# A planned attention and feed-forward kernel: transfers become work of two servers, three pairs' sums go by way of rows in memory, and the ranks are new

## The chip, the core and the metric

The kernel runs on one core of a Trainium2 chip. The metric is the device time of one execution in microseconds; lower is better. A core has five engines that each run their own list of instructions in order: PE (matrix products), DVE (vector), ACT (activation functions), POOL (a slower vector engine that here issues the weights' transfers) and SP (it computes nothing here and issues the other transfers). 16 DMA engines carry the data of all queues.

## The reference, cut to what matters

```python
# q, k, v: (8, 8, 576, 64) float32; moe_w_in: (512, 2048), moe_w_out: (2048, 512), float64
scores = (q @ k.T) / 8
thresh = scores.max(-1) - tau
scores = where(scores >= thresh, scores, -1e9)
attn   = exp(scores - scores.max(-1)); attn /= attn.sum(-1) + 1e-9
x      = (attn @ v)                    # put together to (4608, 512)
h      = x @ w_in
out    = (h * sigmoid(1.702 * h)) @ w_out
```

## The kernel before

**Pairs and blocks.** The 64 heads are 32 pairs, numbered 0 to 31; four pairs make the 512 columns of one batch's x. The feed-forward part takes blocks of 256 tokens. The first two blocks use plain products (`mm1_0`, L754, and `mm2`, L735); blocks from 2 on use products of a fast matrix scheme (`mm1` and `product`); the last four have a scheme of their own.

**What happens to a pair n.**
1. SP loads q and k (`load_qk`, L359) and v (`load_v`, L372). DVE transposes q and k (`prep`, L474).
2. PE makes nine score tiles (`scores`, L489), ACT copies each out of PSUM (`keep`, L506), two to a stored tile, so that a pair has four full tiles and a half one.
3. DVE takes maxima (`in_groups`, L512, once for each tile; `over_tiles`, L522; `over_halves`, L532). For all pairs but pair 2 the row of thresholds is then turned (`turn_rows`, L551), written to device memory by SP (`row_out`, L563) and read back spread over the partitions (`row_in`, L571). Pair 2 is spread by DVE (`spread_max`). Below, "the row's trip" is the way from `row_out` to the landing of `row_in`.
4. DVE subtracts the row from each tile (`sub`, L578); ACT masks it (`mask`, L584) and takes exponentials (`exps`, L588).
5. PE multiplies by v (`values`, L607). The sums of the exponentials of pairs 0 to 4 come from PE (`sums_by_pe`, L615, and `one_row`, L628); from pair 5 on DVE adds them (`in_groups` again, then `over_tiles`). For pairs 5 to 7 DVE then brings them into place and spreads them (`one_group`, L639, and `spread_sums`, L681); from pair 8 on they take a trip through memory like the maxima (`turn_sums`, L653, `sums_out`, L665, `sums_in`, L672).
6. DVE multiplies and puts the result into x (`place_x`, L691).

**Weights.** They come as float64 and are turned into float32 on the chip, in 32 pieces, 16 of `moe_w_in` and then 16 of `moe_w_out`. POOL issues two copies of each piece (L428, the words, and L429, the same bytes shifted by three), DVE cuts out the exponent (`cv_ex`, L437) and the fraction (`cv_frac`, L449, two instructions), ACT makes the power of two (`cv_power`, L444), DVE multiplies both (`cv_end`, L462). A piece needs a staging place, and the place comes free with the `cv_end` of an earlier piece: among the pieces of `moe_w_out` there are one place that pieces 16, 19, 22 and 25 use in turn, and two that the others alternate between. The first six loads wait for `hold` of pair 2 or 3, which follows that pair's `prep`.

**What orders the work.** Nothing is ordered by a scheduler on the chip. A planner in Python (`run_in_order`, L243) plays the program through: a list of tasks, each with an engine, a cost, a rank, the tasks that it comes after, the buffers that it takes and gives back, and a lag (the time after its end at which other engines see it). An idle engine takes the ready task of the lowest rank. A task's rank is its pair's number plus a bias from a table by the function's name (`EARLY` for pairs 0 to 3, `SECOND` for 4 to 7, `LATER`, and `CV` for the weights). The order that comes out is the order of issue, so a wait at the head of an engine's list holds all that is behind it. Before, a transfer is a task of the engine that issues it, with a long lag for the flight: 9.0 for a weight piece, 3.3 and 5.2 for the two halves of a row's trip, 3.0 to 10.0 for q and k.

**First feed-forward product.** `mm1_0` of hidden block 0 can start when `place_x` of pairs 0 to 3 is done and weight pieces 0 to 3 are converted. From there PE has feed-forward work to fill the time between attention work. The planner holds feed-forward products at the lowest priority and gates the scores of pair n by them.

Of the kernel before, what the change touches and what calls it, by code (L numbers as in the profile page):

```python
# [10 lines left out]
FP32 = mybir.dt.float32  # L11
# [3 lines left out]
AF = mybir.ActivationFunctionType  # L15
ALU = mybir.AluOpType
# [3 lines left out]
P = 128  # L20
# [10 lines left out]
def kernel(  # L31
# [84 lines left out]
    stop = const.tile([P, 1], FP32, name="stop")  # L116
    shift = const.tile([P, 1], FP32, name="shift")
# [9 lines left out]
    for x in ("raw0", "raw1", "qkT0", "qkT1", "mb"):  # L127
# [6 lines left out]
        "exps": -11.47,  # L134
        "in_groups": 5.75,
        "keep": 10.66,
        "load_qk": -0.27,
        "load_v": 4.86,
        "mask": -2.66,
        "one_group": -15.86,  # L140
        "one_row": 12.67,
        "over_halves": -7.01,
        "over_tiles": -4.01,
        "place_x": -17.11,
        "prep": -11.73,
        "row_in": 20.49,
        "row_out": 4.47,
        "scores_run": 12.45,
        "spread_max": -1.73,
        "spread_sums": 7.14,  # L150
        "sub": 9.27,
        "sums_by_pe": 0.27,
        "sums_in": -9.39,
        "sums_out": 2.13,
        "turn_rows": -12.55,
        "turn_sums": -0.41,
        "values": 14.64,
        "w_sum": 4.11,
        "x_sum": -14.1,
    }  # L160
    SECOND = {
        "exps": -7.29,
        "in_groups": 20.95,
        "keep": 16.67,
        "load_qk": -8.88,
        "load_v": 5.53,
        "mask": 2.36,
        "one_group": 2.55,
        "one_row": -2.71,
        "over_halves": -12.07,  # L170
        "over_tiles": 2.86,
        "place_x": -20.26,
        "prep": 3.49,
        "row_in": -19.42,
        "row_out": -24.08,
        "scores_run": -7.99,
        "spread_max": -3.11,
        "spread_sums": -2.29,
        "sub": 14.98,
        "sums_by_pe": 35.93,  # L180
        "sums_in": 7.43,
        "sums_out": 4.05,
        "turn_rows": -3.84,
        "turn_sums": 4.03,
        "values": 11.79,
        "w_sum": -10.45,
        "x_sum": -10.98,
    }
    LATER = {
        "exps": 2.01,  # L190
        "in_groups": 10.37,
        "keep": -0.02,
        "load_qk": -6.6,
        "load_v": 3.77,
        "mask": 14.79,
        "one_group": 4.78,
        "one_row": -14.98,
        "over_halves": 1.09,
        "over_tiles": -6.27,
        "place_x": -0.34,  # L200
        "prep": 2.34,
        "row_in": 4.02,
        "row_out": 2.64,
        "scores_run": -11.25,
        "spread_max": -9.44,
        "spread_sums": -6.73,
        "sub": 2.14,
        "sums_by_pe": 1.46,
        "sums_in": 3.78,
        "sums_out": 2.16,  # L210
        "turn_rows": 12.26,
        "turn_sums": 0.29,
        "values": -10.38,
        "w_sum": 6.61,
        "x_sum": 6.02,
    }
    CV = {
        "cv_end": -8.05,
        "cv_ex": 2.22,
        "cv_frac": -11.72,  # L220
        "cv_power": -4.72,
        "load_w": -7.79,
    }

    LAG = {"PE": 0.26, "DVE": 0.18, "ACT": 0.22, "POOL": 0.18}

    QUARTERS = ("scores", "scores_run", "values", "sums_by_pe")
# [12 lines left out]
    FIRST, LAST = -9.0, 1000.0  # L240
    need, follows = {}, {}

    def run_in_order():  # L243
# [12 lines left out]
        while events:  # L256
# [18 lines left out]
            for engine, queue in ready.items():  # L275
                if engine in busy:
                    continue
                for rank, i in sorted(queue):
# [25 lines left out]
    JOINT = 7  # L304

# [183 lines left out]
    def scores(n, j):  # L489
# [8 lines left out]
        if j == NK - 1:  # L498
            del mats[n, 0], mats[n, 1]
# [32 lines left out]
    def over_halves(n):  # L532
        r = stats[n, ALU.max]
        o = work.tile([P, QB], FP32, name="fold", tag="fold", bufs=1)
        for x in (1, 3) if n in BY_DMA else range(4):
            nc.vector.tensor_scalar(
                out=o[ts(x ^ 1, 32)], in0=r[ts(x, 32)], scalar1=gap[ts(x, 32)], scalar2=None,
                op0=ALU.subtract,
            )
        if n in BY_DMA:  # L540
# [10 lines left out]
    def turn_rows(n):  # L551

        nc.vector.transpose(out=flat[1], in_=flat[0])

# [23 lines left out]
    def sub(n, t):  # L578
        s = sT[n, t].rearrange("p u h s -> p u (h s)")
        nc.vector.tensor_tensor(  # L580
# [26 lines left out]
    def values(n, tiles):  # L607
# [4 lines left out]
        if n < NPAIR:  # L612
            free_scores(n, tiles)
# [333 lines left out]
    nc.gpsimd.memset(ones, 1.0)  # L947
    nc.gpsimd.dma_start(
# [26 lines left out]
    BY_PE = 5  # L975
    BY_DMA = (0, 1, *range(3, NP))
    SUMS_BY_DMA = range(8, NP)
    LEAD = 6
    WHOLE = 6

    FFU = 1.727
    T_RANK = FIRST

    W_RANK = (0, 12.87, 12.51, 22.24, 0, 4.97)
    ready_w, w_loads, w64 = [], [], 0
    for i in range(len(pieces)):
# [10 lines left out]
        a = task("POOL", 1.1, rank, load_w, i, after=w_loads[-1:], take=place, lag=9.0)  # L997
        w_loads.append(a)
        e = task("DVE", 0.345, rank, cv_ex, i, after=[a])
        m = task("ACT", 0.67, rank, cv_power, i, after=[e])  # L1000
        a = task("DVE", 1.1, rank, cv_frac, i, after=[e])

        over = [ready_w[y] for y in range(i) if i >= n_in and stage(y) == (i - n_in) // PER_STAGE]
        ready_w.append(task("DVE", 0.61, rank, cv_end, i, after=[a, m] + over, give=place))
# [191 lines left out]
    for n in range(NP):  # L1196
# [5 lines left out]
        slow = 1.1 if n < NPAIR else 1.0  # L1202
# [3 lines left out]
        cost = 3.5 if NPAIR <= n < 2 * NPAIR else 2.0  # L1206
        lag = (4.6, 3.0)[n] if n < 2 else 10.0 if n < 2 * NPAIR else 3.0
        lq = task("SP", cost, r - 2.0, load_qk, n, 0, q0, after=behind, take=own(n, "raw0"), lag=lag)
        lk = task(
            "SP", cost if n else 0.1, r - 2.0, load_qk, n, 1, q1, after=behind,  # L1210
            take=own(n, "raw1"), lag=lag,
        )
        v_m = f"v_m{n % 2}"
        lv = task("SP", 2.4, r + (1.85 if n < 2 else -1.2), load_v, n, after=lvs[-1:], take=(v_m,), lag=3.0)
# [161 lines left out]
```

## Time and profile before

| What | us |
|---|---|
| median of 3 runs (lowest to highest) | 1318.74 (1318.22 to 1318.92) |
| profiled execution, its own time | 1317.94 |
| its span, first to last instruction | 1316.2 |
| PE busy in the span | 1260.9 |
| DVE busy | 1006.1 |
| ACT busy | 646.6 |
| POOL busy | 249.0 |

The profiled execution lies 0.80 us under the median, and 1.74 us of it are outside the span. The page splits the span into 40 slices of 32.9 us and gives each engine's busy share of a slice in tenths. The view by windows gives the same in microseconds for stretches that one names. The timeline gives instructions in order of time, with the idle time in front of them and what ended it in brackets. An engine name with a q (SPq, POOLq) is the engine's sequencer, which issues transfers.

### The profile page before, as it was taken

What the parts mean: (1) busy time and instruction counts of PE and PEld (TensorE: products, weight loads), DVE (VectorE), ACT (ScalarE), POOL (GpSimd) and SP (SyncE); (2) the same over time, 40 slices, a digit from 0 to 9 for tenths busy, and PEclk for the clock granted to TensorE, in tenths of its full rate; (3) what the DMA queues carried; (4) which work ended last, traced back from release to release, by engine and by line L of the source; (5) the groups of instructions that cost most, each with busy time, mean ns of one, the idle gap of its engine ahead of it and who ended that gap; (6) DMA issues with size and microseconds to landing.
All of it is one profiled execution on the core that took longest, in us unless ns stands there. A gap on an engine that the chain in (4) does not pass through costs nothing. (4 is left out here: it accounts for less than half of the span.)

```text
span 1316.2 us, 22807 instructions
## 1 busy us (share of the span) xinstructions
PE 1260.9 (96%) x9128; PEld 975.6 (74%) x9128; DVE 1006.1 (76%) x1610; ACT 646.6 (49%) x830; POOL 249.0 (19%) x291
## 2 busy tenths in 40 slices
PE   5669999999999999999999999999999999999998
PEld 2346864457887777777778888777777778888887
DVE  7989999898888887788777877777888863652642
ACT  4876666576554555555554555454556540210210
POOL 1201211012031211213021303030212117120120
PEclk8879999999999999999999999999999999999999
DMA  8976766545323223212213222323122110000000
GB/s 152 293 189 207 230 207 149 112 77 100 85 55 71 55 55 71 51 50 54 58 42 72 55 71 55 71 55 71 36 55 54 36 46 8 9 1 25 8 0 32
DMA packets 258819, 102.88 MB, mean 78 GB/s; under 512 B 233754, under 2 KB 243994, under 8 KB 258714
## 3 DMA queue, kind: packets, MB, share of 16 engines
q1 hardware_dynamic: 244986, 63.40, 22.4%
q0 software_dynamic: 11360, 37.74, 9.3%
q8 instruction: 71, 1.16, 0.4%
q10 hardware_dynamic: 2368, 0.30, 0.2%
q14 instruction: 34, 0.28, 0.1%
HBM read 87.51 MB, written 9.69 MB: 74 GB/s over the span
## 5 line engine op out<-in xcount | busy, mean ns | idle before, releaser
L516 DVE TRANSPOSE_TENSOR_REDUCE part<-arena 128x36 f32<-128x1152 f32 (+1 forms) x295 | 357.5, 1235 | 41.9 <-ACT arena L510 32.4
L718 PE MATMUL hps<-xT,w_in 128*128 128x256 f32 x1536 | 337.2, 380 | 0.5 <-DVE arena L730 0.4
L718 PEld LDWEIGHTS hps<-xT,w_in 128*128 128x128 f32 x1536 | 290.7, 190 | 45.9 <-issue 5.7
L586 ACT ACTIVATE arena<-arena 128x1152 f32<-128x1152 f32 (+1 forms) x160 | 169.4, 1059 | 144.0 <-DVE arena L580 143.8
L510 ACT COPY arena<-ps 128x576 f32<-128x576 f32 x288 | 170.7, 647 | 115.3 <-PE ps L493 111.9
L580 DVE TENSOR_TENSOR arena<-arena 128x1152 f32<-128x1152 f32 (+1 forms) x158 | 201.1, 1313 | 20.5 <-DMA arena<-row 20.5
L909 PE MATMUL ops<-w_out,arena 128*128 128x256 f32 x896 | 202.4, 380 | 1.8 <-DVE arena L730 1.8
L590 ACT ACTIVATE arena<-arena,shift,scl 128x1152 f32<-128x1152 f32 (+1 forms) x160 | 200.3, 1252 | 4.1
L493 PE MATMUL ps<-arena 64*64 64x288 f32 x2304 | 174.7, 420 | 22.9 <-DVE arena L477 15.3
L909 PEld LDWEIGHTS ops<-w_out,arena 128*128 128x128 f32 x896 | 169.3, 190 | 28.7 <-DVE arena L730 3.1
L875 POOL TENSOR_TENSOR arena<-arena 128x256 f32<-128x256 f32 x56 | 49.7, 888 | 647.1 <-DVE arena L730 543.9
L601 PE MATMUL pv<-arena 64*64 64x288 f32 x2176 | 159.7, 408 | 0.0
L727 ACT ACTIVATE th<-hps 128x512 f32<-128x512 f32 x112 | 66.0, 589 | 186.0 <-PE hps L718 171.8
L909 PE MATMUL ops<-arena 128*128 128x256 f32 x672 | 150.7, 380 | 0.7 <-DVE osb L931 0.7
L493 PEld LDWEIGHTS ps<-arena 64*64 64x64 f32 x2304 | 84.0, 137 | 90.8 <-ACT arena L510 30.4
L909 PEld LDWEIGHTS ops<-arena 128*128 128x128 f32 x672 | 127.1, 190 | 20.4 <-issue 2.2
L601 PEld LDWEIGHTS pv<-arena 64*64 64x64 f32 x2176 | 82.1, 134 | 54.1 <-issue 10.0
L931 DVE SCALAR_TENSOR_TENSOR osb<-ops,osb 128x256 f32<-128x256 f32 x98 | 39.3, 413 | 97.9 <-PE ops L909 90.6
L730 DVE SCALAR_TENSOR_TENSOR arena<-th,hps 128x512 f32<-128x512 f32 x96 | 64.2, 669 | 46.7 <-ACT th L727 46.4
L740 PE MATMUL ops<-w_out,arena 128*128 128x512 f32 x128 | 57.2, 600 | 3.2 <-DVE w_out L465 2.2
L758 PE MATMUL hps<-xT,w_in 128*128 128x256 f32 x256 | 56.4, 381 | 0.0
L888 POOL TENSOR_TENSOR arena<-arena 128x512 f32<-128x512 f32 x28 | 35.6, 1272 | 108.3 <-PE ops L909 108.3
(115 smaller groups left out, 1044.7 us busy)
## 6 DMA issues: line engine op xcount, KB each, us to landing
arena<-in_v_dram SPq DMA_DIRECT2D x128, 144.0 KB
arena<-in_q_dram SPq DMA_DIRECT2D x128, 72.0 KB
out_dram<-osb SPq DMA_DIRECT2D x36, 256.0 KB
arena<-in_k_dram SPq DMA_DIRECT2D x124, 72.0 KB
arena<-row SPq DMA_DIRECT2D x62, 144.0 KB
arena<-row_s SPq DMA_DIRECT2D x48, 144.0 KB
w_out<-in_moe_w_in_dram POOLq DMA_DIRECT2D x12, 512.0 KB, 9.5
arena<-in_moe_w_out_dram POOLq DMA_DIRECT2D x12, 512.0 KB, 6.3
```

Of the source, the lines that this page charges most:

```text
L493: nc.tensor.matmul(ps[ts(c, KT), h, 0:SH], lhsT=mats[n, 1][ts(h, D), ts(j, KT)], rhs=mats[n, 0][ts(h, D), ts(c, SH)], start=True, stop=True,)
L510: nc.scalar.copy(out=sT[n, t][:, u], in_=pss.pop((n, j))[:, :, 0:SH])
L516: nc.vector.tensor_reduce(out=stats[n, op][:, t * 2 * QB : min(2 * t + 2, NK) * QB], in_=sT[n, t].rearrange("p u h (g d) -> p (u h g) d", ...
L580: nc.vector.tensor_tensor(out=s, in0=s, in1=mbs[n].unsqueeze(1).to_broadcast(list(s.shape)), op=ALU.subtract)
L586: nc.scalar.activation(out=s, in_=s, func=AF.Prelu, alpha=STEEP)
L590: nc.scalar.activation(out=s, in_=s, func=AF.Exp, scale=scl, bias=shift)
L601: nc.tensor.matmul(o[c][ts(h, D), 0:SH], lhsT=left(j, h)[ts(c, KT)], rhs=sT[n, t][ts(c, KT), u, h, :], start=(j == 0), stop=(j == NK - 1),)
L718: nc.tensor.matmul(hidden[j][:, ts(f, BLK)], lhsT=w_in[:, c, ds((f * HF + j) * P, P)], rhs=xTs[blk][:, c, :], start=(c == 0), stop=(c == N ...
L727: nc.scalar.activation(out=ths[j], in_=hidden[j], func=AF.Tanh, scale=GELU_SCALE / 2)
L730: nc.vector.scalar_tensor_tensor(out=g[:, :, j, :], in0=two(ths.pop(j)), scalar=1.0, in1=two(hidden.pop(j)), op0=ALU.add, op1=ALU.mult,)
L740: nc.tensor.matmul(acc[i], lhsT=g0[:, j, ts(i, P)], rhs=w_out[:, j, :], start=(j == 0), stop=(j == NFC - 1),)
L909: nc.tensor.matmul(banks[blk][k][:, ts(o, HM)], lhsT=left[:, j, :], rhs=right[:, j, :], start=(j == 0), stop=(j == HF - 1),)
```

## The change

1. The planner gets two more servers, `DMS` for the transfers that SP issues and `DMW` for the weights. A transfer is now an issuing task with a short lag plus a task on its server, taken in order of issue (`for rank, i in queue if engine in MOVERS`), with its own time and a lag of 1.7. The two servers don't slow each other. The steps on the servers issue nothing (`moved` is empty).
2. The planner's times for the weight conversion are a little longer.
3. `SUMS_BY_DMA` begins at pair 5 instead of 8: pairs 5, 6 and 7 lose `one_group` and `spread_sums` and gain `turn_sums`, `sums_out` and `sums_in`.
4. All tables of ranks have new values, so that the order on every engine changes up to about pair 10 and in details after it.
5. Two constants, `minus` and `own_row`, are filled by POOL at the start (two memsets, then four times a memset and an affine select), ahead of the load of `tau`. They serve a second way to mask (`TWICE`), which is empty, as is `BY_POOL`; the functions of that way (`row_blocks`, `again`, `mask_one`) are never called and are left out here.

The sets of tasks on PE, ACT and POOL are the same as before. DVE has three tasks fewer, SP six more.

```diff
-    LAG = {"PE": 0.26, "DVE": 0.18, "ACT": 0.22, "POOL": 0.18}
+    LAG = {"PE": 0.26, "DVE": 0.18, "ACT": 0.22, "POOL": 0.18, "SP": 0.1}
...
+    MOVERS = ("DMS", "DMW")
+
+    def moved():
+        pass
+
+    def transfer(by, time, a, give=(), lag=1.7):
+        return task(by, time, FIRST, moved, after=[a], give=give, lag=lag)
...
-                for rank, i in sorted(queue):
+                for rank, i in queue if engine in MOVERS else sorted(queue):
...
+    nc.gpsimd.memset(minus, 0.0)
+    nc.gpsimd.memset(own_row, 0.0)
+    for x in range(4):
+        nc.gpsimd.memset(minus[ts(x, 32), x % 2, :], -1.0)
+        nc.gpsimd.affine_select(
+            out=own_row[ts(x, 32)], in_=own_row[ts(x, 32)], compare_op=ALU.not_equal, fill=1.0,
+            base=-(QB // 2) * (x // 2), pattern=[[-1, QB // 2]], channel_multiplier=1,
+        )
...
-    BY_PE = 5
+    SUMS_BY_PE = (0, 1, 2, 3, 4)
     BY_DMA = (0, 1, *range(3, NP))
-    SUMS_BY_DMA = range(8, NP)
+    SUMS_BY_DMA = range(5, NP)
...
-    W_RANK = (0, 12.87, 12.51, 22.24, 0, 4.97)
+    W_RANK = (14.85, 6.27, 17.01, 17.33, 8.05, 0.19)
...
-        a = task("POOL", 1.1, rank, load_w, i, after=w_loads[-1:], take=place, lag=9.0)
+        a = task("POOL", 1.1, rank, load_w, i, after=w_loads[-1:], take=place)
         w_loads.append(a)
-        e = task("DVE", 0.345, rank, cv_ex, i, after=[a])
+        a = transfer("DMW", 4.0, a)
+        e = task("DVE", 0.42, rank, cv_ex, i, after=[a])
         m = task("ACT", 0.67, rank, cv_power, i, after=[e])
-        a = task("DVE", 1.1, rank, cv_frac, i, after=[e])
+        a = task("DVE", 1.14 + SHARED, rank, cv_frac, i, after=[e])
...
-        lq = task("SP", cost, r - 2.0, load_qk, n, 0, q0, after=behind, take=own(n, "raw0"), lag=lag)
+        lq = task("SP", 2.1, r - 2.0, load_qk, n, 0, q0, after=behind, take=own(n, "raw0"))
...
+        lq, lk = (transfer("DMS", 3.2, a) for a in (lq, lk))
...
+        lv = transfer("DMS", 2.2, lv)
...
-            a = task("SP", 0.6, r, row_out, n, after=[a], lag=3.3)
-            m = task(
-                "SP", 1.0, r, row_in, n, after=[a], take=own(n, "mb"), give=("row",),
-                lag=5.2,
-            )
+            a = transfer("DMS", 0.3, task("SP", 0.65, r, row_out, n, after=[a]))
+            spread[n] = task("SP", 1.1, r, row_in, n, after=[a], take=own(n, "mb"))
+            m = transfer("DMS", 0.9, spread[n], give=("row",))
...
+            if n in SUMS_BY_DMA:
+                a = task("DVE", 1.35, r, turn_sums, n, after=[a], take=("row_s",))
+                a = transfer("DMS", 0.3, task("SP", 0.65, r, sums_out, n, after=[a]))
+                a = task("SP", 1.2, r, sums_in, n, after=[a], take=("rc",))
+                summed[n] = transfer("DMS", 0.9, a, give=("row_s",))
```

The order that the change gives (task names with the pair or piece; `|` parts what follows before and after):

```
DVE, from the maxima of pair 1 to the row of pair 3
before: ... in_groups 1 | over_tiles, over_halves, turn_rows 1 | prep 3 | in_groups 2 (4 tiles) |
        sub 0 (2 tiles) | weights 0, 1, 2 with sub 0 (3 tiles) between | sub 1 | weights 3 to 6 with the
        sums of pair 0 | maxima of pair 2 | in_groups 3 with sub 2 between | turn_rows 3
after:  ... in_groups 1 | over_tiles 1 | prep 3 with in_groups 2 (4 tiles) | weight 0 |
        over_halves, turn_rows 1 | sub 0 | sub 1 | weight 3 | sums of pair 0 | weights 2, 1, 4, 5 |
        sums of pair 1 | maxima of pair 2 | sub 2 | in_groups 3 with prep 4 between | turn_rows 3
PE, around the first feed-forward products
before: mm1_0 0 to 11 | values 4, sums 4 | mm1_0 12 to 15 with scores 6 | mm2 0 (0 to 6) with scores 6 |
        values 5 with scores 7 | mm2 0 (7) ...
after:  mm1_0 0 to 14 | values 4, sums 4 | mm1_0 15 | mm2 0 (0 to 7) with scores 6 | mm2 1 (0 to 6) |
        values 5 with scores 7 | mm2 1 (7) ...
```

## The prediction, made before any run of the changed kernel

> **What bounds the kernel now.** I read the slices of the span first, then PE's waits, then the timelines around the longest of them.
>
> ```profile
> PE   5669999999999999999999999999999999999998
> DVE  7989999898888887788777877777888863652642
> PEclk8879999999999999999999999999999999999999
> DMA  8976766545323223212213222323122110000000
> ```
> PE is full from the fourth slice on, so the last 1190 us are PE's work and cannot shrink by order alone. Before 120 us PE idles and DVE is full: there the end is set by how soon DVE lets PE begin its feed-forward work. DMA is fullest in the same slices.
>
> ```profile
> 0.00:20.00 20.00, 11.57 (x144) 5.03 (x144) 11.65 (x22) 10.93 (x20) 1.25 (x9) 1.00 0.91 135
> 20.00:40.00 20.00, 7.07 (x76) 3.94 (x80) 19.54 (x27) 9.28 (x14) 6.87 (x14) 0.73 0.86 249
> 60.00:80.00 20.00, 10.05 (x152) 4.82 (x144) 18.78 (x29) 15.45 (x21) 4.23 (x8) 0.84 0.87 248
> 200.00:250.00 50.00, 46.86 (x354) 22.65 (x354) 45.26 (x71) 32.29 (x42) 4.88 (x6) 1.00 0.70 145
> 250.00:300.00 50.00, 47.33 (x375) 26.74 (x374) 46.78 (x72) 35.71 (x44) 5.23 (x5) 0.97 0.43 87
> ```
> The columns after the length are PE, PEld, DVE, ACT, POOL, clock, DMA, GB/s. Up to 120 us PE idles 41.0 us (8.4, 12.9, 4.4, 10.0, 2.8, 2.5 by twenties), from 120 to 400 another 10.5, after that 3.8.
>
> ```profile
> 115.49 2.18 PE L493 MATMUL ps<-arena 64*64 64x288 f32 x32 [0.48 <-DVE xT L703]
> 117.60 1.99 PE L758 MATMUL hps<-xT,w_in 128*128 128x256 f32 x8
> 119.53 0.71 PE L493 MATMUL ps<-arena 64*64 64x288 f32 x8
> 185.88 7.13 PE L740 MATMUL ops<-w_out,arena 128*128 128x512 f32 x16 [0.95 <-DVE arena L764]
> 201.53 1.12 PE L740 MATMUL ops<-w_out,arena 128*128 128x512 f32 x2 [0.60 <-DVE w_out L465]
> 211.98 0.72 PE L493 MATMUL ps<-arena 64*64 64x288 f32 x8 [0.91 <-ACT arena L510]
> 215.38 20.01 PE L740 MATMUL ops<-w_out,arena 128*128 128x512 f32 x46 [1.63 <-DVE w_out L465]
> 271.23 1.78 PE L493 MATMUL ps<-arena 64*64 64x288 f32 x16 [2.16 <-ACT arena L510]
> ```
> Feed-forward begins at 117.60 with one score tile (0.64) still to come: 118.2 in effect. From there to its first block-2 product at 280.23 PE names 6.4 us of waits, on gelus, converted weights and copies.
>
> **The skill.** Trainium skill, DMA: Bandwidth & Descriptors, "Queues, rings and completion order": the queues of SP and POOL share the same DMA engines and are served in turn, packet by packet. The trace agrees. These are the rows' trips of pairs 0 and 3, and what waited for them:
>
> ```profile
> 23.50 0.86 SPq L566 DMA_DIRECT2D row<-flat  x2
> 26.20 1.13 SPq L575 DMA_DIRECT2D arena<-row  x2
> 34.67 2.63 DVE L580 TENSOR_TENSOR arena<-arena 128x1152 f32<-128x1152 f32 x2 [0.23 <-DMA arena<-row]
> 82.19 0.71 SPq L566 DMA_DIRECT2D row<-flat  x2
> 88.56 2.63 DVE L580 TENSOR_TENSOR arena<-arena 128x1152 f32<-128x1152 f32 x2 [3.70 <-DMA arena<-row]
> ```
> Beside the weight loads a trip took 11.2 us (23.50 to 34.67), in a quiet stretch 6.4. Same page, "Anatomy of one DMA": about 2 us of a transfer is fixed (stated for POOL's path; the rows go by SP's, so 4 us for two transfers is an estimate); that leaves 2.4 of the quiet trip for issue and bytes, in line with the issue times shown. Trainium skill, TensorE: Matmul & The Clock Gate, Part 1: an idle PE falls to half its clock. The clock of 0.73 at 20 to 40 us agrees; it makes early idle time a little dearer, and I count nothing for it.
>
> **Prices** (starts of one instruction to the next, DVE timeline): a maximum, sum or subtraction of a full tile 1.27, half tile 0.66, so 5.74 for a pair; `prep` 0.70; `over_tiles` 0.46, `over_halves` 1.04 (pair 2: 1.32), `turn_rows` 0.16, `spread_max` 0.72; a weight 0.33 + 1.08 + 0.62 = 2.03; `one_row`, `spread_sums`, `place_x` 1.09 + 1.00 + 0.87 = 2.96; `one_group` 1.49, `turn_sums` 1.39. ACT masks and exponentiates a pair in 11.2 (49.83 to 61.05). A plain feed-forward task is 1.73 on PE.
>
> **Part 1, the start to `place_x` 3.** I walk the new order with these prices from the old start. Pair 0's row now has both `prep` 1 in front, and ends at 20.2 (19.5 before). Pair 1's maxima and `prep` 2 end at 26.7, 0.9 late; the first tile of pair 2 then has to wait for its two copies (before 2.9 us from product to copy) until 29.9, and with `prep` 3 the four tiles end at 35.7. The exponent and fraction of weight 0 now stand in front of the row of pair 1: its load is issued 0.9 later than before (26.9) and lands at about 36.8 (before, its exponent was cut at 37.2 without a wait), so they end at 38.2 and `turn_rows` 1 at 39.4. Before, that row was ready at 28.7. Pair 0's subtractions and a `cv_end` carry DVE to 45.8. The row of pair 1 leaves at 39.5 among weight loads 0 to 5; with the busy trip of 11.2 it lands at 50.7. **So DVE stands 4.9 us at `sub` 1**, a wait that the planner's 6.5 us trip hides exactly. Then, in order: `sub` 1 56.4, weight 3 57.8, sums 0 60.8, weights 2, 1, 4, 5 and three `cv_end` 68.3, sums 1 71.3, two `cv_end` 72.5, rest of maxima 2 75.7, `sub` 2 81.4, `in_groups` 3 with `prep` 4 88.6, `turn_rows` 3 90.2. The quiet trip ends at 96.6; sums 2 and weights 6, 7 (6.4) cover it. `sub` 3 102.4; ACT ends pair 3 at 98.2 + 11.2 = 109.4, copies scores of pair 5 for `values` 3 until 113.2, and `place_x` 3 ends at 115.3 (before 115.35). But all of pair 5's scores end at 116.2 instead of 118.2, and DVE owes fewer weights only by 2.7 us of its own sum (97.6 of work to this point, before 100.3). **Gain 2.0.** Both ends: with a quiet trip of row 1 (6.4) 6.8; with one of 15 us, which is 3.8 beyond the slowest seen, a loss of 1.8.
>
> **Part 2, to block 2.** PE's work is the same set: 64 feed-forward tasks (110.5), `values` and sums of pair 4 (9.1), scores 6 (5.1), three pairs' `values` with scores (8.9 each): 151.4, and some 4 us of switches and slower products that the trace shows between 118.2 and 280.2 beside the 6.4 of waits. DVE's sum from `place_x` 3 to `place_x` 7 is 150.1, before 153.9: three pairs save 1.49 + 1.00 - 1.39 = 1.1 each, the rest is order. The trips added for them run on SP; `place_x` 5, 6, 7 come 8 to 11 us of DVE work after `turn_sums`, more than 6.4, so I cost them at nothing (cover gone: 6.4 minus what is left, for each). `sums_in` 7 stands behind a store that waits for the first blocks' fourth output; by the order it is issued about 7 us before DVE asks.
> What gets dear is the weights. The work between the `cv_end` that frees a place and the `cv_ex` of the piece that uses it was never under 10.1 us; it is now 7.2 for pieces 25 and 26, 6.8 for 28 and 29, 5.6 for 30 (0.66 + 0.46 + 1.04 + 0.16 + 2.03 + 1.27), 5.8 for 31. The landing of a piece's second copy (L429, loads from 100 to 210 us):
>
> ```profile
> DMA to landing us min/median/max: 4.4/7.1/10.0
> ```
> plus 0.6 for the issue of the first: 5.0, 7.7, 10.6. At the median DVE stands 0.5 (25), 0.9 (28), 2.1 (30), about 3.7 in sum; the others gain by the shift. Then the last weight is ready at 115.3 + 79.8 + 3.7 = 198.8, and PE wants it (seven tasks into `mm2` 0, scores of 6 between) at 116.2 + 83.4 = 199.6. `values` 5 wants the sums of pair 5 at 213.1, ready 211.8. So PE is just fed, with about 1 us to spare. I let 2.4 of the 6.4 us of waits stay: **gain 4.0**, at best 6.4.
>
> **Part 3, the rest.** From `values` 10 on the PE orders are the same; waits there are 3.8 us with the closing chain, which no order touches: 0, plus or minus 1.5. The ten POOL instructions at the start (six memsets, here 0.10 to 0.15 each, and four affine selects, which nothing shows: 0.2 to 0.7, the latter a POOL addition of 256 elements) put off `tau` by 1.4 to 3.7; it landed near 5.3 and is wanted at 8.3, so 0; cover gone, 0.7, which `in_groups` 0 (waiting for ACT until 11.2) hides.
>
> **Sum.** 2.0 + 4.0 = 6.0. The profiled execution would go from 1317.94 to 1311.9 and its span to 1310.2; on the median, 1318.74 - 6.0 = 1312.7.
>
> **Rivals.** (a) Slower: the weight loads of pieces 22 to 31 land at the slow end, 10.6 after release. DVE then stands 2.8 + 3.4 + 3.8 + 5.0 = 15.0 at pieces 22, 25, 28 and 30, 11.3 more than forecast; 1 is spare, PE loses 10.3: 1323.0. It decides from a landing of about 10.3 on. For it: DMA shares of 0.6 to 0.86 at 120 to 180 us, and little room. Against: the median, and the last loads meet a quieter stretch. (b) The row of pair 1 travels quietly, 6.4 us, because no row is in front of it: 4.8 better, 1307.9. For it: SP has issued nothing since row 0. Against: weight loads 3 to 5 were issued 3 us before. (c) The change doesn't do what it says: PE's waits return at other places, since ACT in its fixed order must copy scores between masks (0.91 and 2.16 above); gain 1.5 in all, 1317.2.
>
> **Numbers.** Forecast 0.48 (own range 1309.5 to 1316), (a) 0.22, (b) 0.13, (c) 0.17. A measurement tells some 0.2%, 2.6 us, from no change. Faster: 0.43 + 0.13 + 0.02 = 0.58; same 0.05 + 0.13 = 0.18; slower 0.24. The range 1307 to 1322.5 takes in (b) and (c), and (a) nearly.
>
> **What would show it.** First feed-forward product near 116, DVE idle some 5 us before `sub` 1 with the row as releaser, `place_x` 3 near 115, waits of DVE on weight loads between 165 and 195 of 2 to 6 us, first block-2 product at 273 to 276 with the attention of pair 8 behind it. Wrong if feed-forward begins after 119, or if PE waits over 6 us for weights, gelus or copies between there and block 2.

## The result, and the profile after

The changed kernel took 1335.83 us (median of 4 runs, 1333.66 to 1339.74) beside 1318.83 for the kernel before: a ratio of 1.0127, interval 1.0098 to 1.0156. It is 17.0 us slower, where 6.0 us faster was forecast. The profiled execution took 1336.23, its span is 1334.5.

The slices of the page of the kernel after:

```profile
PE   5658998989999999999999999999999999999998
DVE  6879998988988888778787777787887874652642
PEclk8878999999999999999999999999999999999999
```
A slice is 33.4 us. PE has eights in the fourth, seventh and ninth slices, up to 300 us, where it had nines, and the clock of the fourth is lower. Three windows of the kernel after, cut at the first feed-forward product and at the first block-2 product; the columns are length, PE busy (matmuls), clock, DMA share, GB/s:

```profile
0.00:125.44 125.44, 77.56 (x1008) 0.85 0.71 183
125.44:289.39 163.95, 155.13 (x1036) 0.99 0.68 177
289.39:1334.50 1045.11, 1031.57 (x7092) 1.00 0.22 50
```
The same three of the kernel before, the first cut as in the prediction 0.64 behind the first product, for the score tile that is still to come:

```profile
0.00:118.24 118.24, 77.24 (x1003) 0.87 0.82 210
118.24:280.23 161.99, 155.57 (x1039) 0.99 0.61 165
280.23:1316.20 1035.97, 1028.14 (x7089) 1.00 0.22 50
```
PE's idle time (length less busy) is 41.0, 6.4 and 7.8 before, and 47.9, 8.8 and 13.5 after. So the 18.3 between the two spans are 7.2 + 2.0 + 9.1; 15.0 of them are PE idling and 3.3 PE busy for longer on the same work, at a mean clock of 0.983 (before 0.987).

PE's timeline of the kernel after, the lines around its longest waits from 95 us on:

```profile
95.11 2.20 PE L505 MATMUL ps<-arena 64*64 64x288 f32 x16 [7.25 <-DVE arena L489]
109.54 2.20 PE L654 MATMUL den<-arena,ones 64*64 64x288 f32 x16 [5.04 <-ACT arena L643]
125.44 34.80 PE L811 MATMUL hps<-xT,w_in 128*128 128x256 f32 x160
162.66 17.53 PE L811 MATMUL hps<-xT,w_in 128*128 128x256 f32 x80 [2.42 <-DVE arena L817]
214.82 14.84 PE L793 MATMUL ops<-w_out,arena 128*128 128x512 f32 x30 [3.77 <-DVE w_out L477]
300.21 5.41 PE L771 MATMUL hps<-xT,w_in 128*128 128x256 f32 x16 [3.39 <-DVE arena L783]
306.91 7.17 PE L771 MATMUL hps<-xT,w_in 128*128 128x256 f32 x32 [1.29 <-DVE arena L783]
```
The wait of 5.04 for ACT's exponentials of pair 3 isn't part of the loss: it is as long in E16 below (5.04), where feed-forward begins 11 us earlier. Every other releaser here is DVE. DVE's timeline of the kernel after says what DVE itself stood for (a stand is time in which an engine waits at the head of its list):

```profile
49.49 5.17 DVE L633 TENSOR_TENSOR arena<-arena 128x1152 f32<-128x1152 f32 x4 [4.29 <-DMA arena<-row]
91.01 0.78 DVE L489 STREAM_TRANSPOSE arena<-arena 128x576 f32<-128x576 f32 x1 [8.96 <-DMA arena<-in_q_dram]
159.99 0.78 DVE L489 STREAM_TRANSPOSE arena<-arena 128x576 f32<-128x576 f32 x1 [2.22 <-DMA arena<-in_q_dram]
211.21 1.36 DVE L633 TENSOR_TENSOR arena<-arena 128x1152 f32<-128x1152 f32 x1 [3.76 <-DMA arena<-row]
294.40 5.17 DVE L633 TENSOR_TENSOR arena<-arena 128x1152 f32<-128x1152 f32 x4 [2.91 <-DMA arena<-row]
```
These are `sub` 1, `prep` 4, `prep` 6, `sub` 5 and `sub` 8, and each waits for a transfer. The first was forecast (4.9). The second, 8.96 at the queries of pair 4, was not, and it is the largest. SP's queue in the kernel after shows how it arises, and a view of SP's waits from 50 to 90 us names what SP stood for:

```profile
54.70 14.65 SPq L389 DMA_DIRECT2D arena<-in_v_dram  x8
69.41 18.28 SPq L378 DMA_DIRECT2D arena<-in_q_dram  x4
87.74 3.44 SPq L378 DMA_DIRECT2D arena<-in_k_dram  x4
```
```profile
SPq L389 <- PE ps L505: 10.4, 2, 9.7
SPq L389 <- PE pv L654: 9.7, 1, 9.7
```
The eight issues of the first line are the values of pairs 2 and 3. Pair 3's need the room of pair 1's values, which PE frees (the view names two of PE's lines for it), so SP stands, and the queries of pair 4 stand behind it. POOL meanwhile issues the weight pieces 7 to 11 (5.2 MB) from 67.6 to 75.6 us. The DMA share in windows of the kernel after (the last column but one; it can come out a little over 1):

```profile
60.00:65.00 5.00, 5.00 (x88) 1.00 0.02 5
70.00:75.00 5.00, 3.27 (x48) 1.00 0.96 279
75.00:80.00 5.00, 1.08 (x12) 0.60 0.99 372
80.00:85.00 5.00, 5.00 (x64) 0.71 1.06 384
```
The DMA engines are empty at 60 to 65, when the queries could have travelled, and full at 70 to 85, when they do. In the kernel before, too, the queries stand behind the values of pair 3, but they go out later, and DVE asks for them later:

```profile
74.58 5.35 SPq L366 DMA_DIRECT2D arena<-in_q_dram  x4
84.09 0.77 DVE L477 STREAM_TRANSPOSE arena<-arena 128x576 f32<-128x576 f32 x1
```
They are used 9.5 us after their first issue, without a wait.

### The profile page after: what moved, and what is told of

Its sections match the earlier page's. It is cut to its first block, busy times and chain, and to the rows that moved or that the text cites. A ratio compares the mean times of both kernels' runs of the same rounds, so it can differ in the third digit from the quotient of the medians.

```text
span 1334.5 us, 22829 instructions
## 1 busy us (share of the span) xinstructions
PE 1264.3 (95%) x9128; PEld 976.6 (73%) x9128; DVE 1007.0 (75%) x1601; ACT 647.1 (48%) x830; POOL 247.5 (19%) x301
## 4 chain that ended last, share of the span: by engine, by line
PE 68%; DVE 13%; DMA 7%; ACT 6%; SPq 5%; issue 2%; DVEq 0%; ACTq 0%
PE ops L962 24%; PE hps L771 17%; PE pv L654 7%; PE ps L505 6%; PE ps L876 4%; DVE part L528 4%; PE ps L962 4%; SPq L378 3%; PE ops L876 3%; PE hps L811 2%; ACT arena L639 2%; ACT arena L643 2%; DVE arena L633 2%; DMA arena<-in_q_dram 2%; DMA row<-flat 2%
## 5 line engine op out<-in xcount | busy, mean ns | idle before, releaser
L528 DVE TRANSPOSE_TENSOR_REDUCE part<-arena 128x36 f32<-128x1152 f32 x295 | 358.8, 1237 | 48.8 <-ACT arena L522 39.4
L489 DVE STREAM_TRANSPOSE arena<-arena 128x576 f32<-128x576 f32 x64 | 46.5, 751 | 22.0 <-DMA arena<-in_q_dram 18.0
```

The source lines that it names most:

```text
L528: nc.vector.tensor_reduce(out=stats[n, op][:, t * 2 * QB : min(2 * t + 2, NK) * QB], in_=sT[n, t].rearrange("p u h (g d) -> p (u h g) d", ...
```

## The experiments

All 18 run beside the kernel before (1317.3 to 1318.2 in their medians), so the gap to it is what compares them; the kernel after has +17.0. The last three columns are the stretches of the profiled span, cut as above (0.64 behind the first product where a score tile is still to come: in the kernel before, E5, E7, E10, E12, E14 and E18).

| Run | Edit | Median | Ratio (95 %) | Start | Middle | Rest |
|---|---|---|---|---|---|---|
| before | | 1318.83 | | 118.2 | 162.0 | 1036.0 |
| after | | 1335.83 | 1.0127 (1.0098 to 1.0156) | 125.4 | 164.0 | 1045.1 |
| E1 | after, `prep` 4 late | 1335.52 | 1.0145 (1.0122 to 1.0168) | 126.5 | 170.9 | 1044.8 |
| E2 | after, gelu first | 1339.51 | 1.0175 (1.0151 to 1.0198) | 128.7 | 167.0 | 1046.3 |
| E3 | E1 and E2 | 1337.00 | 1.0148 (1.0135 to 1.0162) | 122.2 | 164.0 | 1047.0 |
| E4 | after, weights behind keys 4 | 1334.28 | 1.0124 (1.0111 to 1.0137) | 119.4 | 168.4 | 1045.0 |
| E5 | before, sums by rows | 1319.24 | 1.0007 (0.9994 to 1.0020) | 118.6 | 161.1 | 1035.4 |
| E6 | before, new ranks | 1354.45 | 1.0273 (1.0248 to 1.0297) | 121.4 | 195.1 | 1036.4 |
| E7 | after, old ranks | 1348.13 | 1.0227 (1.0205 to 1.0248) | 134.1 | 170.8 | 1039.0 |
| E8 | after, one server | 1348.22 | 1.0226 (1.0205 to 1.0248) | 144.9 | 164.1 | 1037.9 |
| E9 | after, half weights | 1325.26 | 1.0046 (1.0028 to 1.0064) | 115.5 | 160.8 | 1043.8 |
| E10 | before, half weights | 1317.77 | 1.0005 (0.9989 to 1.0020) | 114.8 | 164.6 | 1036.8 |
| E11 | after, small sums | 1331.52 | 1.0092 (1.0073 to 1.0110) | 125.1 | 167.3 | 1039.2 |
| E12 | before, small sums | 1313.96 | 0.9958 (0.9944 to 0.9972) | 119.0 | 158.1 | 1035.0 |
| E13 | after, both cuts | 1314.73 | 0.9974 (0.9962 to 0.9985) | 117.6 | 158.2 | 1039.4 |
| E14 | before, both cuts | 1312.24 | 0.9955 (0.9943 to 0.9967) | 114.6 | 160.2 | 1035.2 |
| E15 | after, sums behind keys 10 | 1332.61 | 1.0102 (1.0084 to 1.0120) | 125.0 | 164.0 | 1039.0 |
| E16 | after, keys 4 ahead of values 3 | 1331.51 | 1.0091 (1.0070 to 1.0111) | 114.4 | 163.5 | 1045.3 |
| E17 | E15 and E16 | 1322.01 | 1.0044 (1.0024 to 1.0064) | 115.8 | 163.4 | 1039.1 |
| E18 | before, sums behind rows | 1314.49 | 0.9972 (0.9963 to 0.9981) | 118.1 | 158.2 | 1035.3 |

A single profiled execution of one order varies: the start of the kernel after took 125.4, that of E2, whose order is the same up to block 2, 128.7. Single stretches are read with this 3 us in mind. The profiled execution is one of those timed, and not always a middle one: it is the slowest of its kernel in E1, E4, E11 and E13, and the quickest in E3, E7, E9 and E16.

**E1 to E4: is it the place of the stand?** In kernels that move tasks, the planner's order is kept in a list, the named tasks are moved in it, and then it is issued. E1 and E2, and E3 with both:

```diff
+        move(  # E1
+            lambda f, *a: f in ("prep", "scores_run", "keep") and a[0] == 4,
+            lambda f, *a: f == "turn_rows" and a[0] == 3,
+        )
...
+        move(  # E2
+            lambda f, *a: f in ("sub", "mask", "exps") and a[0] == 8,
+            lambda f, *a: f == "gelu" and a[0] == 0,
+        )
```

> The kernel after, with one edit: the second half's preparation of pair 4 (its transposes, its scores and its masked keys) is issued behind the turn of pair 3's rows, and nothing else moves. Theory (the planner places this preparation directly behind a load of queries that shares the DMA engines with five pieces of weights, and VectorE stands 9.0 us for it): that stand falls under 1 us, the turn of pair 3's rows ends near 90, the first feed-forward product comes near 117 to 119 instead of 125.4, and the time falls by 6 to 9 us, to 1327 to 1330. Rival (the row of pair 3 is what sets the end of part 1, and its trip through memory grows by what is won): the row comes back late, VectorE stands 4 us or more at pair 3's subtraction, and the time falls by 3 us or less. Rival (the ranks, not this place): no change.

> The kernel after, with one edit: the subtractions of pair 8 that stand ahead of block 2's first activation on VectorE, with their masks and exponentials, are issued behind that activation. Theory (they wait for the row of pair 8, whose trip takes 11.4 us beside the accumulating transfers, and TensorE stands behind them for the activation): TensorE's waits of 3.4 and 1.3 us for the activation at 297 to 300 go, the stretch of 289 to 400 loses 4 to 6 us, and the time is 1330 to 1332. Rival (the stand only moves, since pair 8 is needed soon behind it): a wait of like size appears within the next 30 us, and the time changes by 1.5 us or less.

> Both edits of the two kernels before this one in one kernel: the preparation of pair 4 behind the turn of pair 3's rows, and block 2's first activation ahead of the subtractions of pair 8. Theory: the two stands lie in different stages and add, 12 to 14 us together, so the time is 1322 to 1325, with 3 to 6 us still above the kernel before. Rival (the second stand is a consequence of the first, since transfers shift with it): the gain is that of the larger edit alone.

All three missed: none gains. In E1 DVE still stands 3.46 at the queries and 1.36 at the keys of pair 4: this time the issues of pair 3's values lasted into the weights, and the queries behind them went out only at 83.0. The task was moved, the transfer stayed late. (E3 has the same move; there the stands are 1.35 and 0.68 and the start is 3.2 shorter than in the kernel after, and the median is no better.) In E2 the waits for the first activations vanish and one of 6.36 appears at 312.93, PE's timeline of E2:

```profile
312.93 9.46 PE L786 MATMUL hps<-xT,w_in 128*128 128x256 f32 x32 [6.36 <-DVE arena L798]
```
So the rival of E2 was right in what it says happens: the work behind the late row is needed soon after, and moving a task past a stand only moves the stand. (That E2 is slower by 5 us more isn't explained; its order up to block 2 is that of the kernel after.) The theory that the place of these tasks makes the loss fell; what was left was the lateness of the transfers. E4 takes the bytes out of the queries' way:

```diff
+        move(
+            lambda f, *a: f == "load_w" and 7 <= a[0] <= 11,
+            lambda f, *a: f == "load_qk" and a[:2] == (4, 1),
+        )
...
+        if i == 7:
+            nc.gpsimd.tensor_copy(out=stop, in_=raws[4, 1][:, 0:1])
```

> The kernel after, with the loads of weight pieces 7 to 11 issued behind the landing of pair 4's keys (a one-column copy on the POOL engine waits for it), everything else in place. Theory (the load of pair 4's queries is slow only because five pieces of weights, 5.2 MB, share the DMA engines with it): the queries land within 8 us of their issue, the stand of 9.0 us at the preparation of pair 4 falls under 1.5 us; the weights then run beside pair 3's row and may stretch its trip from 6 to 11 us, so the time falls by 3 to 8 us, to 1328 to 1333. Rival (the load is slow by itself, from its many small pieces on the SP queue): the stand stays above 5 us and the time is unchanged or longer.

The queries go out at 71.4 and their four issues take 2.25 instead of 18.28, the stand at `prep` 4 is gone and the start is 6.0 shorter, so the weights did slow the queries. But the gap stays at 17.0. The held weights now cross other loads: DVE stands 4.74 at the queries of pair 6 (2.22 in the kernel after) and PE 6.00 for an activation behind it, and the middle is 4.5 longer. A collision was moved, not taken away.

**E5 to E8: which part of the change?** E5 replaces `one_group` and `spread_sums` of pairs 5 to 7 in place. E6 and E7 exchange the five tables of ranks; E8 is one word.

```diff
     def one_group(n):
+        if n >= 5:
+            return turn_sums(n)
...
     def spread_sums(n):
+        if n >= 5:
+            sums_out(n)
+            return sums_in(n)
...
-        a = transfer("DMW", 4.0, a)
+        a = transfer("DMS", 4.0, a)
```

> The kernel before with one part of the change alone: the sums of pairs five to seven by rows, in place, so that the order of all other work stays as the planner of before wrote it. Theory (the order that the new plan writes costs the time, the sums by themselves do not): 1315 to 1319, within 0.2 % of the kernel before. Rival (the sums by rows cost it, since their row goes out and comes back through memory and VectorE meets it too early): PE's waits behind the sums of pairs five to seven grow and the time is 1322 or more.

> The kernel before, its planner and its sums unchanged, with the new ranks alone. Theory (the planner's new model of transfers is what places work behind loads that are late on the chip): the old model with ranks that weren't searched for it gives a plan that is somewhat worse, 1319 to 1328, still below the kernel after. Rival (the new ranks carry the loss whatever the model): 1332 or more, and with the ranks of before the kernel after falls back under 1325.

> The kernel after, its planner and its sums unchanged, with the ranks of before. Theory (the model of transfers is to blame): 1328 or more, since the model stays. Rival (the ranks are to blame): under 1325. The stands to look at: VectorE at the preparation of pair 4, at the row of pair 1 and at the row of pair 8, with PE's idle time up to the first feed-forward product, from there to block 2, and behind it.

> The kernel after with one edit in its planner: the weights' transfers are counted on the same server as SP's transfers, so that a load behind weights is planned to land late; ranks and everything else as in the kernel after. Theory (a plan that reckons with the sharing does not put the preparation of pair 4 right behind its load): the stand of 9.0 us there falls under 4, and the time lies at 1318 to 1330. Rival (the loads are late in any order, since the bytes of the first 130 us are what they are): the stand moves to another load, and the time is 1332 or more.

E5: the sums by rows cost nothing that can be told, as forecast for the trips. E6 and E7: old planner with new ranks is 37 us slower than the kernel before, new planner with old ranks 31, both worse than the kernel after. Neither ranks nor model carries the loss alone: of the four combinations each planner does best with the ranks that came with it. E6 missed, as it was to stay below the kernel after; E7 lies where its theory put it, but E6 takes that theory's ground away. The long rest of the kernel after (1045.1) belongs to the one order that model and ranks give together: it is 1039.0 with the same model and other ranks (E7), and 1037.9 with the same ranks and another model (E8). In E8 `prep` 4 doesn't wait, as expected, but the time missed: the ranks, made for another model, give an order in which PE waits 14.4, 10.4 and 21.8 us for exponentials before 127 us, and the start takes 144.9.

**E9 to E14: how much of it is transfers?** Two cuts take bytes away and leave the order as it is.

```diff
-        nc.gpsimd.dma_start(
-            out=t3.rearrange("p c w -> p (c w)").bitcast(U8)[:, 0 : 8 * WC - 3],
-            in_=dram.bitcast(U8)[:, 3 : 8 * WC],
-        )
-        cv[i] = t[:, :, 1], t[:, :, 0], t3[:, :, 0]
+        cv[i] = t[:, :, 1], t[:, :, 0], t[:, :, 1]
...
-        nc.gpsimd.dma_start(out=o, in_=a, accum_op=ALU.add)
+        nc.gpsimd.dma_start(out=o[:, 0:1], in_=a[:, 0:1], accum_op=ALU.add)
```

> The kernel after with half of the weights' bytes: of the two copies that each piece is loaded in, the second (shifted by three bytes, from which the fraction is cut) isn't loaded, and the fraction is cut from the first copy, so that the low bits of the weights are left out of the computation; every instruction but the 32 loads stays. Theory (in the kernel after the loads of SP come late because they share the DMA engines with the weights, which its plan does not reckon with): the stands of 9.0 at pair 4's queries and of 4.3 at pair 1's row shrink to 3 and 2 or less, the first feed-forward product comes at 114 to 118, and the time is 1319 to 1326; together with the same edit in the kernel before, the distance of the two shrinks from 17 to 10 or less, most of what is left lying behind block 2's first product. Rival (it is the order of work on the engines, not the transfers): the distance stays at 14 or more.

> The kernel before with half of the weights' bytes, by the same edit as in the run ahead of this one (the low bits of the weights are left out). Theory: its order meets late transfers at few places (3.7 at pair 3's row, 2.2 at weights), so it gains 3 to 7 us, to 1310 to 1314. Rival (the engines' work, not the transfers, sets the end): 2 us or less.

> The kernel after with the four accumulating transfers of the weights' sums (1 MB each, on the POOL queue) cut to a quarter of their bytes, so that three quarters of these sums are left out of the computation. Theory (around 285 to 305 they stretch the trip of pair 8's row to 11.4 us and the load of pair 10's keys): VectorE's waits of 2.9 and 2.7 there fall under 1 each, PE's waits for block 2's activations (3.4 and 1.3) under 1.5 in sum, and the time falls by 3 to 6 us, to 1328 to 1332. Rival (SP's own loads for pair 10 and the rows crowd each other): the waits stay and the time changes by less than 2 us.

> The kernel before with the same four transfers cut to a quarter of their bytes (three quarters of the sums are left out). Theory: in the order of before nothing on the path waits for what shares the engines with them, so 0 to 1.5 us, 1315.5 to 1318. Rival (these transfers cost both kernels alike): 3 us or more, to 1314 or less.

> The kernel after with both cuts: half of the weights' bytes (the low bits of the weights left out) and a quarter of the four accumulating sums' bytes (three quarters of the sums left out). Theory (two collisions of transfers make nearly the whole loss: SP's loads with the weights before 125 us, and the row of pair 8 with the sums at 285 to 305): first feed-forward product near 115.5, first block-2 product near 276, and 1039 to 1040 from there, so 1315 to 1319, which is 2 to 6 above the kernel before with the same cuts. Rival (a loss of 8 us or more lies in the order of work on the engines): 1322 or more.

> The kernel before with both cuts (low bits of the weights and three quarters of the sums left out). The weights' cut alone gave it 0 and the sums' cut alone 4: 1312 to 1315 if they add, under every theory; it is there so that the kernel after with the same cuts has its like.

E9 came as the theory said: `prep` 4 stands 1.34, `sub` 1 1.97, feed-forward begins at 115.5 and the gap to E10 is 7.5 instead of 17. E10 missed (0 instead of 3 to 7), as its rival said: its start is 3.4 shorter and its middle 2.6 longer. E11 has the stands at pair 8's row and pair 10's keys gone and the rest 5.9 shorter, and its gap is 3.6 smaller; the middle of its trace is 3.3 longer. E12 missed, and its rival was right: the kernel before gains 4.2, of which 3.9 lie in the middle. So with the sums alone made small in both kernels the gap is 17.6 (1331.52 and 1313.96), no smaller than 17.0: the sums cost the two alike, at different places. With both cuts the two kernels stand at 1314.73 and 1312.24: **the gap of 17.0 shrinks to 2.5** (E13 came 0.3 below its range). So 14.5 of it go with the bytes of these two kinds of transfer, in unchanged orders and with DVE's conversion steps as long as before: 9.5 with the weights alone, the other 5.0 with the sums only once the weights are lighter. The spans (1315.2, the slowest of E13's nine runs, and 1310.0) differ by 3.1 - 2.0 + 4.2 in the three stretches.

**E15 to E18: the two collisions one by one, in the full computation.** E16 moves one load on SP's queue, E15 the last two accumulating sums; E17 has both. E18 gives the kernel before the like of E15, for its second and fourth sum.

```diff
+        move(  # E15
+            lambda f, *a: f == "t_plus" and a[0] >= 2,
+            lambda f, *a: f == "load_qk" and a[:2] == (10, 1),
+        )
...
+        if x == 2:  # E15
+            nc.gpsimd.tensor_copy(out=stop, in_=raws[10, 1][:, 0:1])
...
+        move(  # E16
+            lambda f, *a: f == "load_v" and a[0] == 3,
+            lambda f, *a: f == "load_qk" and a[:2] == (4, 1),
+        )
...
+        move(  # E18
+            lambda f, *a: f == "t_plus" and a[0] == 1,
+            lambda f, *a: f == "row_in" and a[0] == 7,
+        )
...
+        if x == 1:  # E18
+            nc.gpsimd.tensor_copy(out=stop, in_=mbs[7][:, 0:1])
+        if x == 3:  # E18
+            nc.gpsimd.tensor_copy(out=stop, in_=mbs[9][:, 0:1])
```

> The kernel after, full computation, with the last two accumulating sums issued behind the landing of pair 10's keys (a one-column copy on the POOL engine waits for it). Theory (they stretch the trip of pair 8's row): VectorE's wait of 2.9 for that row falls under 1 and PE's waits of 3.4 and 1.3 under 1.5 in sum, from the first block-2 product to the end 1039 to 1041 instead of 1045, so the time falls by 3 to 6 us where the stretch ahead is as before. Rival (pair 10's loads alone stretch the trip): PE's waits stay, 1 us or less.

> The kernel after, full computation, with one load moved on SP's queue: the values of pair 3 are issued behind the queries and keys of pair 4 instead of ahead of them. Theory (the queue stands 9.7 us at the values of pair 3, which wait for a room that PE frees, and the queries behind them then meet the weights): queries and keys of pair 4 are issued near 57 and land by 66, the stand of 9.0 us at their preparation goes, the first feed-forward product comes at 115 to 119 instead of 125.4, and the time falls by 4 to 8 us. Rival (the values of pair 3, later by this, then stop pair 3 itself): PE waits for them between 95 and 115 and the gain is 2 us or less. Rival (what is won is lost again at the weights, as it was when the weights were held back): the first product is early, but block 2 begins less than 3 us earlier than 289.

> The kernel after, full computation, with both moves: pair 4's queries and keys ahead of pair 3's values on SP's queue, and the last two accumulating sums behind the landing of pair 10's keys. Theory (two separate collisions): the profiled execution has its first feed-forward product near 115, its first block-2 product near 278 and 1039 to 1041 from there, so a span of 1317 to 1320 where the run is one of the quick ones, and the median lies at 1318 to 1327, nearer the upper end, as the first move alone had runs from 1325 to 1334. Rival (the gains do not add): the median stays at 1329 or more.

> The kernel before, full computation, with the second accumulating sum issued behind the landing of pair 7's row and the fourth behind that of pair 9's row (a one-column copy on the POOL engine waits for each). Theory (the second sum stretches the trip of pair 7's row, and VectorE stands 3.6 us for it): that stand goes, block 2 begins near 277 to 278 instead of 280.2, and the time is 1313.5 to 1316, below both kernels. Rival (the sums then meet the row or the loads of the next pair): 1316.5 or more.

SP's queue in E16, to be set against the three lines of the kernel after:

```profile
54.11 2.70 SPq L404 DMA_DIRECT2D arena<-in_v_dram  x4
56.86 2.24 SPq L393 DMA_DIRECT2D arena<-in_q_dram  x4
59.14 2.12 SPq L393 DMA_DIRECT2D arena<-in_k_dram  x4
65.31 2.73 SPq L404 DMA_DIRECT2D arena<-in_v_dram  x4
```
The queries go out at 56.9, before any of the weight pieces 7 to 11, their four issues take 2.24 instead of 18.28, DVE doesn't stand at `prep` 4, and feed-forward begins at 114.4, 11.0 earlier. All of the gain is in the start (the table has the stretches), and none is lost later in this execution (1324.97). But the timed runs go from 1324.97 to 1333.80 with a median of 1331.51; the trace shows the quickest of them. The gap is 13.6, 3.4 less than that of the kernel after, and short of the 4 to 8 expected. In E15 the stands at pair 8's row are gone and the rest is 1039.0, as expected, and the profiled execution is 6.5 below that of the kernel after; the gap is 2.3 smaller, less than the 3 to 6 expected. E17's median is 1322.01, inside what was expected: 12.9 of the 17.0 are won back by moving one load and two sums. That is more than the 3.4 and 2.3 of the single moves; the runs of each kernel spread over 7 to 10 us, and what makes the sum so unequal isn't shown. E18 came as expected: block 2 begins at 276.3, the stand of 3.58 at the row of pair 7 is gone, and 1314.49 is below both kernels (0.9972, interval 0.9963 to 0.9981). So with sums moved in both, the new order (E17) is still 7.5 above the old one.

## Why the prediction was wrong, step by step

The forecast for the three stretches was -2.0, -4.0 and 0; they moved by +7.2, +2.0 and +9.1. Both signs of being wrong that it named came: feed-forward began after 119, and between there and block 2 PE waits 8.8 for activations, weights and copies.

- **Part 1, up to `sub` 2: right.** `turn_rows` 0 ended at 20.1 (20.2), weight 0 at 37.6 (38.2), `turn_rows` 1 at 38.9 (39.4); the row of pair 1 took 10.6 from issue to use (11.2), DVE stood 4.29 there (4.9), and `sub` 2 began at 74.9 (75.7). That the stand came so near is in part luck: in E2, with the same order up to there, it was 7.73.
- **Part 1, "`in_groups` 3 with `prep` 4 88.6": this step failed.** It costs `prep` 4 as work alone, and asks for no transfer. The walk checked the landing of weights and rows, but not that of the queries. The new order asks for them at 82.1 and ahead of the row of pair 3, so that a wait holds this row too; the kernel before asks at 84.1, behind it. DVE stood 8.96, `turn_rows` 3 ended at 98.6 instead of 90.2, and feed-forward began at 125.4 instead of 116.2. With the queries out of the weights' way it began at 114.4 (E16) and 115.5 (E9): the rest of the walk held within 2 us. The Trainium skill, DMA: Bandwidth & Descriptors, "Queues, rings and completion order", says that the queues share the DMA engines; the trace agrees with it here too (the four issues of the queries take 18.28 beside the weights and 2.25 where these are held back, E4), and I applied it to the weights and rows only.
- **The planner makes the same mistake.** By its costs a load of queries takes 2.1 + 0.1 + 3.2 + 1.7 = 7.1 from its issue, and the plan has it issued at 73.2 and `prep` 4 at 80.4, with nothing to spare; on the chip it took 21.6 (69.41 to 91.01). In the plan `DMW` and `DMS` don't slow each other, and the change also took away a margin: the old planner allowed 3.5 + 10.0 = 13.5 for this load and 0.6 + 3.3 + 1.0 + 5.2 = 10.1 for a row's trip, which the new one puts at 6.55. A trip with no weights under way took 6.4, those beside weights or sums 10.5 to 11.6. So the new costs fit a transfer that travels alone, and the old ones left room for one that doesn't. No run gives the new planner the old margins, so what this alone does isn't shown.
- **Part 2, gain 4.0: wrong in the waits.** The middle is 2.0 longer, not 4.0 shorter. The weights' landing, on which rival (a) turned, is not what ends it, and DVE stands at no weight piece there: it stands 2.22 at pair 6's queries (PE 2.42 behind it) and 3.76 at pair 5's row, beside the last two weight pieces, and the last `cv_end` stands behind that (PE 3.77). "I cost them at nothing" held for the sums' trips (E5), but the trip of the maxima's row of pair 5 took 10.5. With light transfers in both kernels the middle is 158.2 (E13) against 160.2 (E14): 2.0 of the 4.0 were there, and the same kind of collision took them. (A slip without weight: the stands at pieces 25, 28 and 30 add up to 3.5, not 3.7.)
- **Part 3, "0, plus or minus 1.5": wrong by 9.1.** I held that closing waits are all that is left once PE's order is the same. DVE's order and the moment of transfers are not: the row of pair 8 left at 282.80, at the same time as the third accumulating sum of 1 MB (283.05), and DVE had it 11.6 later. Four `sub` 8 stand for it ahead of the first activation, and PE idles: it is busy 1.82 of the 5 us from 295 on, and its clock from 300 to 305 is 0.66. Moving the sums takes 6.1 off the rest (E15). Some 3 remain against the kernel before; what they are is open.
- **The rivals.** (a) named a slower outcome by late weights; the outcome was slower, the cause a different transfer. (b), a quiet trip of row 1, didn't come. (c), ACT's waits returning, holds for 2.28 at 268 us, a small part.
- **POOL's constants: right.** Affine selects took 0.19 each, `tau`'s load went out 1.5 later, and nothing waited.

What stays open: why the runs of E16 spread over 9 us, and why E15 and E16 give so much more together than alone. The traces show a load that scatters, the queries of pair 6 beside weights, at which DVE stood 2.0 (E16), 2.2 (after), 4.1 (E11), 4.7 (E4) and 6.5 (E1); whether that makes the spread isn't shown, since there is no trace of E16's slower runs. Open too is why the kernel before gains nothing from half the weights' bytes.

## What to carry to other kernels

For each instruction that a change moves earlier, ask when the transfer that it reads was issued, what stands ahead of that transfer on its queue, and what the other queues move at that time. A stand that is a late transfer isn't cured by moving the work that waits: start the transfer in an idle stretch, or take bytes out of its way and see what they meet next. Where a plan's costs are made to fit a transfer that travels alone, ask which margin the old costs held for those that don't. And ranks found with one planner were worth nothing with the other (E6 and E7: 37 and 31 us slower than the kernel before).

## What was not expected of the hardware

- A load of 288 KB of queries in four transfers took 2.24 us to issue ahead of the weights (E16), 2.25 with the weights held back (E4), and 18.28 beside five weight pieces: the issue itself stretches, so all that is behind it on SP waits too.
- A row's trip was 6.4 us with no weights under way, and 10.5 to 11.6 beside weight loads or one accumulating sum of 1 MB: a trip of a few KB out and 288 KB back, nearly doubled.
- Leaving out one of the two copies of all weights (32 of some 512 KB) was worth 10 us to one order and nothing to another of the same work.
